# Transposes of norms and of A's outputs by the DMA engines, two residual buffers and an even split of Wo in a four-layer kernel

## The chip, the cores and the metric

The kernel runs on one core of one Trainium2 chip. The metric is the device time of one execution in microseconds; lower is better. Engines are named as in the profile: PE (TensorE matmul), PEld (its weight loads), DVE (VectorE), ACT (ScalarE), POOL (GpSimd), SP (SyncE, which only issues DMAs here). SPq and ACTq are the queues on which SP and ACT issue DMAs.

## The reference

A residual stream x of 2048 tokens and 640 channels passes through four layers, A, B, A, B, each after a layer norm without weights:

```python
x = A_x
x = x + _A_ref(_layernorm(x), A_wq, A_wk, A_wv, A_wo, A_beta)
x = x + _B_ref(_layernorm(x), B_mem0, B_Wq, B_Wk, B_Wv, B_Wo, B_seg_len)
x = x + _A_ref(_layernorm(x), A_wq, A_wk, A_wv, A_wo, A_beta)
x = x + _B_ref(_layernorm(x), B_mem0, B_Wq, B_Wk, B_Wv, B_Wo, B_seg_len)
```

Layer A has 32 heads of 20 channels and four segments of 512 tokens. In each segment every head does causal softmax attention inside the segment, and reads a memory M, z of the segments before through phi(q) M / (phi(q) z + 1e-6), with phi(t) = t + 1 for t > 0 and exp(t) else. A gate per head mixes the two; after that the segment's phi(k), v are added to the memory. The concatenated heads are multiplied by wo.

Layer B is recurrent: 64 steps of 32 tokens. A step puts 8 memory rows in front of its 32 tokens, projects all 40 rows to q, k, v of 32 heads of 128 channels, does masked softmax attention over the 40 rows, and multiplies by Wo (32 x 128 x 640). The first 8 output rows are the memory of the next step, the other 32 are the step's output. So step s + 1 cannot begin its memory part before step s has ended.

## The kernel before, in words

**Layer A** is cut into 32 units (4 segments n of 8 groups G of 4 heads), and each unit into six slots. In each slot PE computes a part of the scores (tile a_S), ACT takes exp into a_PT, POOL or DVE applies the causal mask to a_PT, and PE multiplies a_PT by the values (a_pv). Into the slots are woven the projections of the next unit (proj, tile a_PP, cast by DVE to a_qk), phi of q and k (phi_q, phi_k; k is turned by PE into a_KN), the memory update (memory), the normalisation of the unit before (norm, which writes 80 columns of the tile a_Onat, on DVE in the first segment and on POOL after it), and, in extras, work at fixed (G, slot) places. That work is: for the next segment, loading 128 rows of x (ln_load), their statistics (ln_stats), the norm (ln_apply, tile a_xn, one buffer), its transpose into a_xnT (ln_tr) and the value projection (vproj); for the segment before, the transpose of its outputs a_Onat into a_oT (chunk, five times) and the output projection (outp, eight times), which adds the residual and stores x in float32 and in bf16. One SBUF tile, a_wvo, holds wv and wo in turn. The PSUM pool pg of two buffers (tag "pg") serves proj, phi_k, memory, ln_tr, vproj, chunk and outp alike.

Both ln_tr and chunk transpose on PE: four or five 128x128 transposes into one PSUM tile, which ACT copies to SBUF.

**Layer B** works step by step. Its passes are Q and K of the memory columns (b_Qa, b_Ka, b_Qb, b_Kb), scores (b_SP), V (b_V), values (b_OTL) and the output pass OPass (b_OPS, 16 pairs of heads in HORDER: heads 0 to 15 first). The parts that do not depend on the memory are computed for four steps at once (TailUnit, tile b_tail; the deferred output pass b_OPSd) and are woven in as filling. The norm of the next 128 tokens is made once in four steps: ln_norm and ln_apply in a step with s % 4 == 2, ln_tr in the step after, again with five PE transposes (b_lntps) and an ACT copy into b_xnTg. The residual rows of a step are loaded into b_XO, one buffer, in the middle of the step; add_out adds the step's output to it on DVE, and store writes it out. For steps with s % 4 == 1 the store is made at the step's end, for the others in the middle of the next step.

Wo lies in two SBUF tiles: b_wo1 with the first NW1 = 11 heads, loaded at the beginning of layer B, and b_wo2 with the other 21, which takes space that layer A's output tiles (a_oT, a_wvo, a_xb and others) give free, and so is loaded after A's last output is stored. At the beginning of B the remaining output work of A (br.tail: the last chunk and eight outp) is woven between the first TailUnits and the first Q and K of step 0.

**Order.** PE, ACT, DVE and POOL execute in the order in which the program is written (the class _OrdNC chains each engine's instructions; its line 85 is therefore the source line of nearly all rows of the profile, and rows are told apart by tiles). DMAs issued through nc_raw.sync or nc.sync are not chained: their order on SP is the framework's scheduler's. The framework also inserts the waits for buffers and for memory that is used again.

## Time and profile before

| | us |
|---|---|
| median of 3 runs | 2297.86 |
| lowest and highest run | 2294.97, 2298.25 |
| profiled execution, its own time | 2302.5 |
| span of the profiled execution, first to last instruction | 2300.8 |
| first A, B, second A, second B (about) | 0 to 293, to 1140, to 1435, to 2301 |
| mean granted clock of TensorE | 0.981 |

A row of a group gives line, engine, operation, tile written <- tiles read (partitions x elements, type), count, then busy us, mean ns of one, and idle time of that engine just before, with what ended it. A row of the timeline gives start, length, engine and operation; in brackets stands the engine's idle time before it and what released it. A row of waits gives total us, number, longest. Matmuls overlap in PE's pipeline, so the duration of one is longer than the time that it costs; that time is read from the starts of two successors.

### The profile page before, as it was taken

The page shows a single profiled execution, that of the slowest core. Times are in us where ns is not written, and L with a number is a line of the kernel's source. Part 1 is how long each engine was busy: PE and PEld are TensorE (multiplying, and loading weights), DVE is VectorE, ACT ScalarE, POOL GpSimd, SP SyncE. Part 2 cuts the span into 40 slices and gives each one's busy share as a digit, 9 for nine tenths or more (in the row PEclk, how much of TensorE's full clock was granted, in tenths as well). Part 3 has the DMA queues.
Part 4 walks back from the last instruction along what each step waited for, and adds up shares of the span by engine and source line. Part 5 has one row for each costly group of instructions (what it writes and reads, how often), then busy time and mean ns, then how long its engine had stood idle before and what let it go on. Part 6 is the DMA issues. An engine that isn't in the chain of part 4 may idle for free.

```text
span 2300.8 us, 123029 instructions
## 1 busy us (share of the span) xinstructions
PE 2195.3 (95%) x54988; PEld 1234.9 (54%) x54988; DVE 1623.6 (71%) x3996; ACT 961.6 (42%) x2207; POOL 1028.5 (45%) x2475
## 2 busy tenths in 40 slices
PE   6998989999999999999889989899999999999997
PEld 3444545555555555555445445455555555555554
DVE  5777757777777777776667777577777777777775
ACT  5777823333333333333267667233323333333332
POOL 3344534444444444444323445344444444444442
PEclk9999989999999999999999999999999999999999
DMA  6455540000000000000123333400000000000000
GB/s 168 138 147 166 164 143 21 20 21 19 20 19 20 20 22 20 22 15 18 49 89 119 105 108 119 147 19 15 18 15 17 16 19 16 17 18 16 14 13 15
DMA packets 90652, 123.40 MB, mean 54 GB/s; under 512 B 16496, under 2 KB 80000, under 8 KB 88192
## 3 DMA queue, kind: packets, MB, share of 16 engines
q1 hardware_dynamic: 87648, 111.84, 16.9%
q8 instruction: 431, 7.06, 1.3%
q10 hardware_dynamic: 2464, 3.61, 0.6%
q14 instruction: 109, 0.89, 0.1%
HBM read 89.17 MB, written 26.21 MB: 50 GB/s over the span
## 4 chain that ended last, share of the span: by engine, by line
PE 81%; DVE 8%; ACT 5%; issue 3%; DMA 2%; SPq 1%; POOL 0%; DVEq 0%; ACTq 0%; POOLq 0%
PE b_V L85 13%; PE b_OPS L85 12%; PE b_tail L85 10%; PE b_Qa L85 6%; PE b_Kb L85 6%; PE b_Ka L85 6%; PE b_Qb L85 6%; PE b_SP L85 5%; PE a_PP L85 4%; ACT a_PT L85 4%; PE b_OTL L85 3%; PE b_OPSd L85 3%; PE a_S L85 2%; PE a_pv L85 2%; DVE a_qk L85 1%
## 5 line engine op out<-in xcount | busy, mean ns | idle before, releaser
L85 PEld LDWEIGHTS <-b_hT 128*32 128x32 bf16 x15120 | 372.3, 96 | 311.3 <-DVE b_hT L85 69.2
L85 ACT ACTIVATE b_PT<-b_SP 128x224 bf16<-128x224 f32 x256 | 92.3, 361 | 765.5 <-PE b_SP L85 744.7
L85 PE MATMUL b_V<-b_wv,b_hT 128*32 128x512 bf16 x5040 | 356.3, 381 | 0.0
L85 ACT ACTIVATE a_PT<-a_S 128x768 bf16<-128x768 f32 (+1 forms) x384 | 326.4, 893 | 62.8 <-PE a_S L85 56.1
L85 PE MATMUL b_OPS<-b_wo,b_OTsb 128*32 128x320 bf16 x8192 | 329.3, 302 | 6.5 <-DVE b_OTsb L85 5.1
L85 PEld LDWEIGHTS <-b_OTsb 128*32 128x32 bf16 x8192 | 200.4, 97 | 94.9 <-DVE b_OTsb L85 47.5
L85 POOL CAST b_QT<-b_TQ 128x384 bf16<-128x384 f32 x254 | 140.3, 552 | 231.5 <-DVE b_TQ L85 231.5
L85 ACT CAST b_OTsb<-b_OTL 128x320 bf16<-128x320 f32 x384 | 150.9, 427 | 198.9 <-PE b_OTL L85 183.1
L85 POOL TENSOR_TENSOR b_PT<-b_PT,b_R 128x64 bf16<-128x64 bf16 x256 | 107.3, 419 | 221.8 <-ACT b_R L85 197.4
L85 POOL CAST b_KT<-b_TQ 128x384 bf16<-128x384 f32 x254 | 142.6, 561 | 136.8 <-DVE b_TQ L85 132.1
L85 PE MATMUL b_Qa<-b_wq,b_hT 128*32 128x512 bf16 x2520 | 183.2, 384 | 5.0 <-DVE b_hT L85 5.0
L85 POOL TENSOR_SCALAR_AFFINE_SELECT a_PT<-a_PT 128x256 bf16<-128x256 bf16 x256 | 108.2, 424 | 174.2 <-ACT a_PT L85 162.1
L85 PE MATMUL b_Kb<-b_wk,b_hT 128*32 128x512 bf16 x2520 | 182.9, 380 | 0.1
L85 PE MATMUL b_Ka<-b_wk,b_hT 128*32 128x512 bf16 x2520 | 182.2, 382 | 0.0
L85 DVE STREAM_TRANSPOSE b_TM<-b_OPS 128x128 f32<-128x128 f32 x252 | 88.2, 350 | 123.6 <-PE b_OPS L85 119.7
L85 PE MATMUL b_Qb<-b_wq,b_hT 128*32 128x512 bf16 x2520 | 158.3, 379 | 0.0
L85 PE MATMUL a_PP<-a_xnT,a_wt 128*128 128x512 bf16 x560 | 146.5, 394 | 5.1 <-DVE a_um L85 1.3
L85 PE MATMUL a_S<-a_qk 32*128 32x512 bf16 (+3 forms) x1024 | 137.2, 308 | 8.1 <-ACT a_PT L85 6.9
L85 DVE CAST b_Vsb<-b_V 128x512 bf16<-128x512 f32 x128 | 88.6, 692 | 76.8 <-PE b_SP L85 48.0
L85 DVE CAST b_OTsb<-b_OTL 128x320 bf16<-128x320 f32 x128 | 62.9, 492 | 98.2 <-PE b_OTL L85 98.2
L85 DVE TENSOR_TENSOR b_PT<-b_PT,b_R 128x160 bf16<-128x160 bf16 x256 | 104.0, 406 | 37.7 <-PE b_V L85 18.6
L85 POOL TENSOR_TENSOR b_Rtot<-b_Rtot,b_R 128x160 bf16<-128x160 bf16 x256 | 126.6, 494 | 0.0
(165 smaller groups left out, 4276.0 us busy)
## 6 DMA issues: line engine op xcount, KB each, us to landing
a_wt<-a_wpad SPq DMA_DIRECT2D x112, 160.0 KB
b_XO<-xres SPq DMA_DIRECT2D x256, 30.0 KB
a_wvo<-in_A_wo_dram SPq DMA_DIRECT2D x8, 800.0 KB
b_wq<-in_B_Wq_dram SPq DMA_DIRECT2D x20, 256.0 KB
b_wk<-in_B_Wk_dram SPq DMA_DIRECT2D x20, 256.0 KB
xres<-a_xo SPq DMA_DIRECT2D x16, 320.0 KB
xres_bf<-a_xb SPq DMA_DIRECT2D x32, 160.0 KB
b_wv<-in_B_Wv_dram SPq DMA_DIRECT2D x20, 256.0 KB
```

Of the source, the lines that this page charges most:

```text
L85: r = f(*a, **k)
```

## The change

The norm's transposes of segments 1 to 3 of A, of the bridge between A and B, and of all of B, and the transposes of A's outputs become DMA transposes issued on SP; the first segment's norms and the transposes of k stay on PE. Loading, statistics, norm and transposes in A start one unit earlier (tt + 1 in place of tt + 2), the five calls of chunk become four of o_turn (one for each 128 tokens, at slots 3 and 4 of the segment's first unit), and outp is moved by about half a unit (from (1, 2) ... (3, 3) to (1, 3) ... (3, 5)). Several tiles go from one pool to another or from two buffers to one. exp of k is written into a_phik itself. B gets two b_XO buffers, loaded at the beginning of a step. NW1 goes from 11 to 16; the load of b_wo1 goes from SP, at B's beginning, to ACT's queue, after A's remaining output work. The first six TailUnits of B run without A's outputs between them, and two outp stand in front of each of the four first Q and K passes.

```diff
 S_TOK = 2048
-NW1 = 11
+NW1 = 16
...
         wk1 = ctx.enter_context(tc.tile_pool(name="a_wk1", bufs=1, reuse_waits="tile"))
+        nat = ctx.enter_context(tc.tile_pool(name="a_nat", bufs=1, reuse_waits="tile"))
...
         xnTs = [st.tile([128, NCH, 512], BF16, name=f"a_xnT{i}") for i in range(2)]
-        Onat = so.tile([128, 4, D], BF16, name="a_Onat")
+        Onat = nat.tile([128, 4, D], BF16, name="a_Onat")
...
 
-        def ln_tr(nc, xn, n, tt):
+        def ln_tr(nc, xn, n, tt, dma=True):
+            dst = xnTs[n % 2][:, :, 128 * tt:128 * tt + 128]
+            if dma:
+                nc_raw.sync.dma_start(dst, xn[:], transpose=True)
+                return
...
                 nc.tensor.transpose(tps[:, c, :], xn[:, 128 * c:128 * c + 128], C.identb[:])
-            nc.scalar.copy(xnTs[n % 2][:, :, 128 * tt:128 * tt + 128], tps[:])
+            nc.scalar.copy(dst, tps[:])
...
             nc.vector.memset(bd[32 * j:32 * j + 32, j, :], 1.0)
-        eps = so.tile([128, 2, 4, 4], F32, name="a_eps")
+        eps = st.tile([128, 2, 4, 4], F32, name="a_eps")
...
             if tt > 0:
-                ln_tr(nc, ln_apply(nc.vector, xts[tt - 1], *stats[tt - 1]), 0, tt - 1)
+                ln_tr(nc, ln_apply(nc.vector, xts[tt - 1], *stats[tt - 1]), 0, tt - 1, dma=False)
...
                 vproj(nc, 0, tt, half, ("dve", "act")[half])
-        gg = W.gates(nc, so)
+        gg = W.gates(nc, st)
...
             us, xin = {}, {}
-            wl = wk1 if general else wk
...
                 U = us[u]
-                t1 = wl.tile([128, 512], BF16, name="a_t1q", tag="t1")
+                t1 = wk1.tile([128, 512], BF16, name="a_t1q", tag="t1")
...
                 KNv = KN[:].rearrange("p t (j s) -> p t j s", s=32)[:, :, :, 0:20]
-                EK = wl.tile([128, 4, 4, 20], BF16, name="a_EK")
-                nc.scalar.activation(out=EK[:], in_=KNv, func=ACT.Exp)
-                t1 = wl.tile([128, 4, 4, 20], BF16, name="a_t1k", tag="t1")
+                pk = phik[u % 2][:, :, :, 0:20]
+                nc.scalar.activation(out=pk, in_=KNv, func=ACT.Exp)
+                t1 = wk1.tile([128, 4, 4, 20], BF16, name="a_t1k", tag="t1")
                 nc.vector.tensor_scalar(out=t1[:], in0=KNv, scalar1=1.0, scalar2=1.0, op0=ALU.add, op1=ALU.max)
-                nc.vector.tensor_tensor(out=phik[u % 2][:, :, :, 0:20], in0=EK[:], in1=t1[:], op=ALU.min)
+                nc.vector.tensor_tensor(out=pk, in0=pk, in1=t1[:], op=ALU.min)
...
                     nc.tensor.transpose(mt[:, qc, :], parts[:, qc].rearrange("p j i -> p (j i)"), C.identb[:])
-                ms = wl.tile([12, 512], BF16, name="a_ms", tag="t1")
+                ms = wk1.tile([12, 512], BF16, name="a_ms", tag="t1")
...
                 pv = us[u].pv
-                r = so2.tile([128, 2, 4, 4], F32, name="a_r")
+                r = wk.tile([128, 2, 4, 4], F32, name="a_r")
                 nc.vector.tensor_tensor(out=r[:, 0:K], in0=pv[:, 0:K, :, :, 20], in1=eps[:, 0:K], op=ALU.add)
-                i = so2.tile([128, 2, 4, 4], F32, name="a_i")
+                i = wk.tile([128, 2, 4, 4], F32, name="a_i")
...
                     watch(nc, C, r[:, 0].rearrange("p t j -> p (t j)"), i[:, 0].rearrange("p t j -> p (t j)"))
-                q = so2.tile([128, 2, 4, 4], F32, name="a_q")
+                q = wk.tile([128, 2, 4, 4], F32, name="a_q")
...
                 else:
-                    ts = so.tile([128, 2, 16, 20], F32, name="a_ts")
+                    ts = wk1.tile([128, 2, 16, 20], F32, name="a_ts")
...
                 else:
-                    um = wk1.tile([128, 4, 21], F32, name="a_um", tag="a_EK" if general else "a_um")
+                    um = wk1.tile([128, 4, 21], F32, name="a_um", tag="t1" if general else "a_um")
...
 
-            def chunk(c):
-                tps = pg.tile([128, 4, 128], BF16, name="a_otps", tag="pg")
-                for tt in range(4):
-                    nc.tensor.transpose(tps[:, tt, :], Onat[:, tt, 128 * c:128 * c + 128], C.identb[:])
-                nc.scalar.copy(oT[:, c, :], tps[:].rearrange("p t q -> p (t q)"))
+            def o_turn(tt):
+                nc_raw.sync.dma_start(oT[:, :, 128 * tt:128 * tt + 128], Onat[:, tt, :], transpose=True)
...
                     xn, m0 = ln["b"]
-                    tps = pg.tile([128, NCH, 128], BF16, name="a_btps", tag="pg")
-                    for c in range(NCH):
-                        nc.tensor.transpose(tps[:, c, :], xn[:, 128 * c:128 * c + 128], C.identb[:])
-                    nc.scalar.copy(br.xnT[:], tps[:])
+                    nc_raw.sync.dma_start(br.xnT[:], xn[:], transpose=True)
+                if (G, slot) == (6, 0):
+                    m0 = ln["b"][1]
+                    mp = wk1.tile([8, D], BF16, name="a_bm0p", tag="a_xn")
+                    nc.vector.tensor_copy(mp[:].rearrange("p (g jj d) -> p jj g d", jj=2, d=32),
+                                          m0[:].rearrange("p (jj g d) -> p jj g d", jj=2, d=32))
+                    ln["b"] = mp
+                if (G, slot) == (6, 3):
...
                     nc.gpsimd.tensor_copy(br.hT[:, :, 32:56], v[:, :, 1, 0:24])
-                    mp = wk1.tile([8, D], BF16, name="a_bm0p", tag="a_xn")
-                    nc.vector.tensor_copy(mp[:].rearrange("p (g jj d) -> p jj g d", jj=2, d=32),
-                                          m0[:].rearrange("p (jj g d) -> p jj g d", jj=2, d=32))
-                    ln["b"] = mp
...
                     if (G, slot) == (0, 0):
-                        chunk(3)
...
                             res_load(n - 1, 0); res_load(n - 1, 1)
-                    elif (G, slot) == (1, 0):
-                        chunk(4)
+                    elif (G, slot) in ((0, 3), (0, 4)):
+                        o_turn(2 * slot - 6); o_turn(2 * slot - 5)
                     else:
-                        seq = [(1, 2), (1, 3), (1, 5), (2, 0), (2, 3), (2, 5), (3, 0), (3, 3)]
+                        seq = [(1, 3), (1, 5), (2, 1), (2, 3), (2, 5), (3, 1), (3, 3), (3, 5)]
...
                     bridge_ops(G, slot)
-                seq = {(4, 0): 0, (5, 0): 1, (6, 0): 2}
-                if (G, slot) in seq:
-                    chunk(seq[G, slot])
...
                     for tt in range(4):
-                        if (G, slot) == (tt + 2, 0):
+                        if (G, slot) == (tt + 1, 0):
                             ln[tt] = ln_load(n + 1, tt)
-                        if (G, slot) == (tt + 2, 5):
+                        if (G, slot) == (tt + 1, 5):
                             ln[tt] = (ln[tt],) + ln_stats(nc, ln[tt])
-                        if (G, slot) == (tt + 3, 1):
+                        if (G, slot) == (tt + 2, 1):
                             ln[tt] = ln_apply(nc.vector, *ln[tt])
-                        if (G, slot) == (tt + 3, 4):
+                        if (G, slot) == (tt + 2, 4):
...
                     row_max(u + 1)
-            br.tail = [lambda: chunk(4)] + [lambda i=i: outp(NS - 1, i) for i in range(8)]
+            br.tail = [lambda i=i: outp(NS - 1, i) for i in range(8)]
...
             xn = ln_n.pop(g)
-            tps = pot.tile([128, NCH, 128], BF16, name="b_lntps", tag="ot")
-            for c in range(NCH):
-                nc.tensor.transpose(tps[:, c, :], xn[:, 128 * c:128 * c + 128], C.identb[:])
             xg = wk2.tile([128, NCH, 128], BF16, name="b_xnTg")
-            nc.scalar.copy(xg[:], tps[:])
+            nc.sync.dma_start(xg[:], xn[:], transpose=True)
...
         xnT_g[0], hT[0], hx[0] = br.xnT, br.hT, br.hx
-        for a, b in ((0, NW1 // 2), (NW1 // 2, NW1)):
-            nc_raw.sync.dma_start(wo[0][:, a:b, :], wo_src[:, a:b, :])
...
             nc.vector.memset(Rtot[:], 0.0)
-        XO = st.tile([64, 320], F32, name="b_XO")
-        nc.vector.memset(XO[:], 0.0)
+        XOs = [st.tile([64, 320], F32, name=f"b_XO{i}") for i in range(2)]
+        for t in XOs:
+            nc.vector.memset(t[:], 0.0)
...
                 flush()
-                if kind != "Q" or b:
-                    tail()
...
             for b in range(2):
+                tail(2)
...
                 place(("act", "pool")[b], turn(ps[:]), b, heads(dst[0]), 0, 24, 0)
-                tail()
         tail(100)
+        for a, b in ((0, NW1 // 2), (NW1 // 2, NW1)):
+            nc.scalar.dma_start(wo[0][:, a:b, :], wo_src[:, a:b, :])
...
         wo.append(wop2.tile([128, 32 - NW1, D], BF16, name="b_wo2"))
-        for a, b in ((NW1, 22), (22, 32)):
+        for a, b in ((NW1, 24), (24, 32)):
...
             T, i4 = divmod(s, 4)
+            XO = XOs[s % 2]
+            for jj2 in range(2):
+                nc.sync.dma_start(XO[32 * jj2:32 * jj2 + 24, :], x_src[32 * s:32 * s + 24, 320 * jj2:320 * jj2 + 320])
...
                 late.pop(0)()
-            for jj2 in range(2):
-                nc.sync.dma_start(XO[32 * jj2:32 * jj2 + 24, :], x_src[32 * s:32 * s + 24, 320 * jj2:320 * jj2 + 320])
...
                 ln_dma((s + 7) // 4)
-            def store(s=s, ops=ops):
+            def store(s=s, ops=ops, XO=XO):
```

## The prediction

> **What bounds the kernel now.** I read the page first, then busy time by stage, then the added and removed tiles one by one, then PE's waits, and last the chain of waits around the two places where a layer A hands over to a layer B. The page gives the span and the bound; the windows split it into layer A, B, A, B:
>
> ```profile
> span 2300.8 us, 123029 instructions
> PE 2195.3 (95%) x54988; PEld 1234.9 (54%) x54988; DVE 1623.6 (71%) x3996; ACT 961.6 (42%) x2207; POOL 1028.5 (45%) x2475
> ...
> 24.00:292.00 268.00, 244.83 (x2768) 130.18 (x2767) 196.36 (x502) 200.31 (x279) 120.94 (x309) 0.97 0.52 149
> 330.00:1138.00 808.00, 801.85 (x23918) 459.29 (x23922) 581.80 (x1418) 266.41 (x796) 374.78 (x897) 1.00 0.08 19
> 1166.00:1435.00 269.00, 245.47 (x2764) 130.23 (x2762) 196.62 (x487) 198.69 (x272) 116.73 (x281) 0.96 0.34 106
> 1476.00:2301.00 825.00, 806.56 (x24056) 465.52 (x24048) 585.30 (x1425) 268.21 (x800) 375.32 (x898) 0.99 0.07 16
> ```
>
> (Columns: stage, length, busy PE, PEld, DVE, ACT, POOL, clock, DMA share, GB/s.) In B, PE is busy 802 of 808 us: an operation taken off PE shortens B by its own length. In A, PE is busy 245 of 268; the other 23 us are short waits on DVE and ACT. So A is bound by PE first, and PE's waits second.
>
> What PE spends on the transposes that leave it, and what it waits in front of them:
>
> ```profile
> L85 PE MATMUL a_tps<-c_identb,a_xn x160: 216/219/315, 10.6 to 1369.4; 128*128 128x128 bf16 x160
> L85 PE MATMUL a_otps<-c_identb,a_Onat x160: 216/219/315, 58.2 to 1438.7; 128*128 128x128 bf16 x160
> L85 PE MATMUL b_lntps<-c_identb,b_xn x150: 218/219/231, 319.6 to 2177.4; 128*128 128x128 bf16 x150
> ...
> 2177.14 0.45 PE L85 MATMUL b_lntps<-c_identb,b_xn 128*128 128x128 bf16 x5
> 2177.53 0.40 PE L85 MATMUL b_V<-b_wv,b_hT 128*32 128x512 bf16 x4
> ...
> 268.29 0.39 PE L85 MATMUL a_otps<-c_identb,a_Onat 128*128 128x128 bf16 x4
> 268.61 0.33 PE L85 MATMUL a_S<-a_qk 32*128 32x384 bf16 x2
> ...
> PE a_otps L85 <- DVE a_vaug L85: 2.3, 6, 0.4
> PE a_tps L85 <- DVE a_vaug L85: 2.3, 4, 0.7
> ```
>
> The durations overlap; the start of the next instruction gives the price: five transposes hold PE for 2177.53 - 2177.14 = 0.39 us, four for 0.32.
>
> What the DMA engines do where the new transposes run:
>
> ```profile
> 1139.96 1.59 DMA b_XO<-xres
> ...
> 1456.17 2.51 DMA xres_bf<-a_xb
> 1459.29 12.72 DMA b_wo<-in_B_Wo_dram
> ...
> 1472.06 1.78 PE L85 MATMUL b_OPS<-b_wo,b_OTsb 128*32 128x320 bf16 x22 [1.28 <-DMA b_wo<-in_B_Wo_dram]
> ...
> 241.82 1.09 POOL L85 TENSOR_TENSOR a_Onat<-a_ts 128x320 bf16<-128x320 f32 x1
> ...
> 248.32 1.08 POOL L85 TENSOR_TENSOR a_Onat<-a_ts 128x320 bf16<-128x320 f32 x1
> ```
>
> A 160 KB transfer takes 2.51 us from issue to landing. The late part of Wo takes 12.7 us, and PE waits 1.28 us for it. Between the last write of a_Onat in one segment and the first of the next there are 248.32 - 242.91 = 5.4 us.
>
> **The change, part by part.**
>
> Transposes off PE. In A, three of four segments' norms go (12 groups of five per layer; the first segment's four stay on PE), so of 32 groups 24 go: 24 x 0.39 = 9.4 us. A's outputs: 160/4 = 40 groups x 0.32 = 12.8 us. The bridge's norm: 2 x 0.39 = 0.8. In B 30 groups x 0.39 = 11.7. Sum 34.7 us of PE, 23.0 in A and 11.7 in B. The Trainium skill (TensorE: Matmul & The Clock Gate, Part 4) puts a 128x128 transpose at 275 to 390 ns, which would make these 440 worth 121 us or more; here they follow each other at about 80 ns, and I take the trace's 34.7.
>
> ACT loses the copies behind them (0.58 us x 40, 0.69 x 54, about 60 us). ACT is not the bound, so they count nothing by themselves. But the transposes share two PSUM buffers (tag pg) with everything else in A, and PE stands in front of them: 2.3 + 2.3 + 1.3 us in the first A (also on a_xo), 3.4 + 1.5 + 1.3 in the second, 12.1 together. DVE is late for the next user of pg too, so I count half: 6 us; bounds 0 and 12.
>
> What is added: 24 + 32 + 2 + 30 = 88 DMA transposes of 128x640, all on SP's queue. No row shows one. From below, each is a plain 160 KB DMA: about 0.4 us of SP (a_wt's two issues take 0.8), landing after 2.5 us, and about 0.5 us behind a predecessor (160 KB at the 362 GB/s of the window 1461 to 1466, where Wo streams). From above, the Trainium skill (VectorE: DVE Perf Modes, The three transpose paths) gives 1309 ns for a 128x128 by DMA against 390 on TensorE, and this speaks against the change: five blocks make 6.5 us each (estimate). By the first, four transposes of A's outputs land after 2.5 + 3 x 0.5 = 4.0 us, inside the 5.4; by the second after 26 us, far outside. I take 1.2 us each behind a predecessor, nearer to the row, because a transfer spread over 16 engines should not serialise its blocks: 2.5 + 3 x 1.2 = 6.1 us.
>
> The waits that this adds. (a) The a_Onat tile has one buffer: the Onat addition of the next segment waits on POOL until all four transposes have read it. There are six such places, four of 5.4 to 5.9 us and two of 8.8 (after a first segment). Behind it on POOL stand the a_PT selects, for which the P*V matmuls wait. At 6.1 us POOL waits 0.5 us four times; its own 45% load hides this. (b) a_xn has one buffer: DVE's next norm waits for the transpose of the last. DVE writes a_xn at 195.14, 204.17 and 213.65, 9 us apart; the transpose may start within this time whenever SP is free, and SP's order has residual stores and loads in front of it. Mostly hidden; behind DVE stand the a_qk casts, and then PE. (c) The output projections start half a unit later, some 7 us after the transposes' issue: hidden. I put 3 us on (a) to (c) at PE. At 2.5 us instead of 1.2 it would be about 10 (the formula is under the first rival).
>
> In-place exp into phik, single t1 buffers, tiles moved between pools: written and read in the order of one engine or a unit apart; DVE and ACT orders hide them; nothing, at most 1 us. The bridge's POOL copies move from (5,4) to (6,3), still a unit before layer B: nothing.
>
> B's residual. With one b_XO buffer the load follows the last store; DVE waits 2.4 us for it in all (five times), and the chain of waits has its 1.59 us in front of the second A. Two buffers, loaded at the step's start, take both away: 3 us. SP's store-then-load wait stays, but hides.
>
> The hand-over. Before, 1,760 KB of Wo are issued at B's start and 3,360 KB after A's last outputs are stored. After, 2,560 KB go on ACT's queue behind A's last output projection and 2,560 on SP as before. So 5.2 MB are in flight at once; at 362 GB/s this is 14.5 us, beginning about a microsecond after the last projection: all of it lands about 16 us after, where it landed 15.6 to 17 us after before (1472 against 1454.7). The first half of the heads is whole in the first part, so the 1.28 us wait may go; but PE also stops 2.6 us for its own instructions in this load (1463.9 to 1466.5, "issue") and 3.4 us at 322, and two bulk queues may lengthen that. ACT's two issues (about 1 us) stand in front of the first b_PT exp, which comes 4 us later. POOL's copy to b_hx now waits for a transpose queued behind Wo on SP; POOL catches up while PE waits for Wo anyway. Net +1 us for both layers; bounds -3 and +10. A's last outputs are covered: four transposes land within some 9 us of the last Onat, and six tail units (3.97 + 4 x 1.19 us of PE) now run in front of the projections.
>
> Sum: 23.0 + 6 + 11.7 + 3 - 3 - 1 = 39.7 us saved. The profiled execution is 2302.5 us (span 2300.8), so 2262.8; it lies 4.6 above the median of the runs, 2297.86, so as a median 2258.
>
> **The rivals.**
>
> Slow transposes. If a DMA transpose takes t behind its predecessor, POOL is held 2.5 + 3t - 5.6 us at four places and 2.5 + 3t - 8.8 at two, less about 2 us of slack. The total is 18t - 37: with 6.5 us it is 80, plus some 15 for DVE's norms; against 43 us of gain the kernel takes about 2350. It turns slower from t = 4.4 us. For it: the skill's figure, the single a_Onat buffer. Against it: the rows of plain DMAs. A milder form, t near 3, costs 17 to 20 and gives 2275.
>
> A is not PE's. If DVE (196 of 268 us) and ACT set the unit's length, the 23 us on PE in A turn into waits on a_qk and a_PT, and only B's 11.7 + 3 and about 6 remain: 2277 too. For it: the rows of waits on DVE casts. Against it: PE's 91% in A.
>
> More than counted. All of the 12 us of waits vanish, and the half-clock stretches in A (clock 0.96 to 0.97) shrink: 34.7 + 12 + 4 + 10 = 61 us, 2237.
>
> **How the numbers follow.** Main case 0.58 (2246 to 2270), more 0.10, the two half gains 0.15, a gain eaten up to within 0.2% 0.05, slower 0.12. A measurement of this kernel tells about 0.2%, 4.6 us, from no change. The range 2234 to 2298 leaves out the slow case and the tail of the fast one. Faster by over 0.2%: 0.83.
>
> **What would show it.** Right: no a_otps and b_lntps rows, B's windows each about 6 us shorter with PE as busy, A's each 12 to 15 shorter, no wait on b_XO. Wrong: waits of POOL a_Onat or DVE a_xn on DMAs, PE b_OPS waiting on b_wo for more than 3 us, a longer PE "issue" at the hand-over, or SP issuing a transpose for over 2 us.

## The result, and the profile after

| | before | after |
|---|---|---|
| runs | 4 | 4 |
| median, us | 2296.49 | 2270.22 |
| lowest and highest, us | 2294.97 to 2298.25 | 2263.58 to 2272.96 |
| profiled execution: span (time), us | 2300.8 | 2271.2 (2272.96) |

The ratio of the medians is 0.9881 with an interval of 0.9856 to 0.9906: the changed kernel is faster by about 26 us. The page of its profile shows that TensorE has 440 matmuls fewer and is as full as it was, and that small packets have multiplied (before: 16496 under 512 B):

```profile
span 2271.2 us, 122201 instructions
PE 2150.9 (95%) x54548; PEld 1206.1 (53%) x54548; DVE 1632.1 (72%) x3998; ACT 907.9 (40%) x2111; POOL 1023.7 (45%) x2475
...
DMA packets 149785, 137.78 MB, mean 61 GB/s; under 512 B 75632, under 2 KB 139136, under 8 KB 147328
```

The stages say where the time came from. These are the windows with the same landmarks in both kernels: the two layers A, from the first matmul of a_PP to that of the last unit, and the two layers B, from the fourth step to the last. Columns: stage, length, busy PE, PEld, DVE, ACT, POOL, granted clock, DMA share, GB/s. First the kernel before:

```profile
24.57:280.42 255.85, 234.53 (x2627) 124.20 (x2625) 188.55 (x484) 189.63 (x265) 114.29 (x292) 0.97 0.54 153
1164.13:1422.34 258.21, 236.48 (x2626) 124.87 (x2625) 189.97 (x472) 187.38 (x259) 110.00 (x264) 0.97 0.35 110
360.90:1130.90 770.00, 764.88 (x22915) 439.47 (x22911) 557.09 (x1355) 255.41 (x762) 361.74 (x866) 1.00 0.08 20
1501.55:2274.94 773.39, 767.66 (x22915) 443.31 (x22911) 557.64 (x1355) 255.52 (x762) 361.70 (x866) 1.00 0.07 16
```

and the changed kernel:

```profile
25.32:269.79 244.47, 223.01 (x2494) 112.10 (x2492) 190.70 (x483) 173.80 (x235) 113.96 (x292) 0.98 0.69 174
1156.05:1388.10 232.05, 220.20 (x2494) 112.03 (x2492) 190.61 (x471) 171.50 (x229) 108.89 (x264) 1.00 0.52 140
356.38:1122.47 766.09, 760.26 (x22844) 439.16 (x22840) 560.20 (x1355) 247.07 (x748) 360.12 (x866) 1.00 0.10 23
1476.55:2242.48 765.93, 759.54 (x22845) 439.99 (x22841) 560.09 (x1355) 246.94 (x748) 360.02 (x866) 1.00 0.09 19
```

Four things are to be seen. The two B lose 3.9 and 7.5 us of length, and 12.7 us of busy PE together. The second A loses 26.2 us, of which PE's busy time gives 16.3 and its idle time 9.9 (258.21 - 236.48 = 21.7 before, 11.9 after), and its clock rises from 0.97 to 1.00. The first A loses only 11.4 us. These gains add up to 49.0 us, and the span fell by 29.6: so about 19 us were given back elsewhere. The place is the two hand-overs: from the last matmul of a_PP to the second step of B it takes 49.5 and 48.8 us before, 56.2 and 58.6 us after (+16.5). The other 3 us are at the end, the start and between the layers.

The new transposes themselves are as quick as the prediction assumed. The row of the tile a_oT (minimum, median, maximum of SP's issue in ns):

```profile
L493 SPq DMA_TRANSPOSE a_oT<-a_Onat x32: 1205/1276/2502, 90.9 to 1408.5; - x32
```

SP is held 1.28 us by each (median), where a plain load of the same size takes 0.43 us; four in a row go out 1.3 us apart, and the packets of the first at 285.40 end 1.9 us after its issue (packets of the trace, matched by time and size).

The waits that belong to the change (waiting engine and tile, what ended the wait, us in all, times, longest):

```profile
POOL a_xb L85 <- DMA xres_bf<-a_xb: 38.0, 9, 6.8
DVE a_st L85 <- DMA a_xt<-in_A_x_dram: 13.7, 6, 6.3
PE b_OPS L85 <- DMA b_wo<-in_B_Wo_dram: 9.7, 4, 4.2
PE b_Kb L85 <- DVE b_TQ L85: 9.5, 2, 6.3
POOL a_Onat L85 <- DMA a_oT<-a_Onat: 8.3, 4, 2.3
```

The wait of POOL on a_Onat is the one that the prediction named; PE waits only 0.6 us in all for POOL's a_PT, which stands behind it. No row of DVE's a_xn waiting for a DMA exists. The other four rows belong to what was given back; those of POOL and DVE count only where PE waits behind them. The chain of waits around the first hand-over tells their order (start, length, what):

```profile
303.63 6.38 DMA xres_bf<-a_xb
...
310.16 0.73 POOL a_xb L85
310.91 4.66 DMA xres_bf<-a_xb
...
316.22 10.60 DMA b_wo<-in_B_Wo_dram
...
326.86 1.28 PE b_OPS L85 x16
```

The third store of a_xb goes out at 303.63, just after ACT has issued 2.6 MB of Wo at 302.48. It lands late, POOL waits for the tile's one buffer, the last store comes later still, the second half of Wo may only start when that store has released the space (315.79), and PE stands in front of b_OPS until it is there. PE's other wait, 6.3 us for DVE's b_TQ, hangs on the same late store: on POOL the norm's b_ln_rstd stands behind a_xb, and DVE's b_xn, which waits for it, stands in front of b_TQ:

```profile
312.23 0.45 DVE L85 TENSOR_SCALAR b_xn<-b_xt,b_ln_mv,b_ln_rstd 128x640 bf16<-128x640 bf16 x1 [5.77 <-POOL b_ln_rstd L85]
```

In the first A there is one place more, here in the timeline:

```profile
157.47 6.28 SPq L493 DMA_TRANSPOSE a_oT<-a_Onat  x4
...
164.89 1.82 SPq L653 DMA_DIRECT2D b_wk<-in_B_Wk_dram  x4
166.76 0.42 SPq L248 DMA_DIRECT2D a_xt<-in_A_x_dram  x1
...
173.60 0.89 DVE L85 BATCH_NORM_STATS2 a_st<-a_xt 128x6 f32<-128x320 bf16 x2 [6.28 <-DMA a_xt<-in_A_x_dram]
...
175.55 0.60 ACT L85 ACTIVATE a_phiq<-a_PP 128x512 bf16<-128x512 f32 x1 [7.89 <-DVE a_qk L85]
```

Four transposes hold SP for 6.3 us, four loads of B's weights (256 KB each) follow, and only then the row block that the next norm needs. DVE waits 6.28 us for it, the cast of a_qk stands behind, and this unit takes 16.3 us where the same unit of the second A takes 9.3.

### The profile page after: what moved, and what is told of

It is laid out like the page before. It is cut to its first block, busy times and chain, and to the rows that moved or that the text cites. A ratio compares the mean times of both kernels' runs of the same rounds, so it can differ in the third digit from the quotient of the medians.

```text
span 2271.2 us, 122201 instructions
## 1 busy us (share of the span) xinstructions
PE 2150.9 (95%) x54548; PEld 1206.1 (53%) x54548; DVE 1632.1 (72%) x3998; ACT 907.9 (40%) x2111; POOL 1023.7 (45%) x2475
## 2 busy tenths in 40 slices
DMA packets 149785, 137.78 MB, mean 61 GB/s; under 512 B 75632, under 2 KB 139136, under 8 KB 147328
## 4 chain that ended last, share of the span: by engine, by line
PE 81%; DVE 7%; DMA 5%; ACT 3%; issue 2%; POOL 1%; SPq 1%; POOLq 0%; DVEq 0%; ACTq 0%
PE b_V L85 13%; PE b_OPS L85 13%; PE b_tail L85 10%; PE b_Kb L85 6%; PE b_Qa L85 6%; PE b_Ka L85 6%; PE b_Qb L85 6%; PE b_SP L85 5%; PE b_OTL L85 4%; PE a_PP L85 3%; PE b_OPSd L85 3%; ACT a_PT L85 2%; PE a_S L85 2%; PE a_pv L85 2%; DMA xres_bf<-a_xb 2%
## 5 line engine op out<-in xcount | busy, mean ns | idle before, releaser
L85 PE MATMUL a_PP<-a_xnT,a_wt 128*128 128x512 bf16 x560 | 141.8, 385 | 10.3 <-ACT a_phiq L85 6.2
L85 DVE STREAM_TRANSPOSE b_TQ<-b_Kb 128x512 f32<-128x512 f32 x128 | 91.7, 716 | 46.0 <-PE b_Kb L85 25.1
```

The source lines that it names most:

```text
L85: r = f(*a, **k)
```

## Experiments

The times of the whole kernel spread by 3 to 14 us within a set of runs, so most verdicts rest on stages of the profiled executions. How well those repeat can be seen from kernels in which a stage was not touched: the second A of the same code (first a_PP to last unit) took 232.0 to 235.4 us in ten executions, and the changed kernel's is the lowest of them; the two B (sum from fourth to last step) took 1531.7 to 1535.9, and the two hand-overs (sum from last a_PP to second step) 109.7 to 114.7 in the changed kernel and in E1, E3 and E4, which leave them alone; here the changed kernel's is the highest. A difference inside such a band proves nothing.

| run | ratio to before (interval) | first A | second A | hand-overs | B, sum |
|---|---|---|---|---|---|
| before | 1 | 259.4 | 261.7 | 98.3 | 1543.4 |
| changed | 0.9881 (0.9856 to 0.9906) | 247.7 | 235.2 | 114.7 | 1532.0 |
| e1_prefetch | 0.9879 (0.9847 to 0.9911) | 238.3 | 235.5 | 109.9 | 1531.7 |
| e6_order | 0.9905 (0.9870 to 0.9939) | 248.6 | 235.5 | 111.2 | 1532.6 |
| e7_wo_early | 0.9924 (0.9902 to 0.9946) | 249.1 | 238.1 | 118.4 | 1533.2 |
| e8_order_wo | 0.9920 (0.9888 to 0.9951) | 248.4 | 237.6 | 115.6 | 1533.2 |
| e10_wo_pieces | 0.9915 (0.9891 to 0.9939) | 250.1 | 237.9 | 115.9 | 1533.2 |
| e11_both | 0.9871 (0.9845 to 0.9896) | 246.4 | 238.1 | 112.8 | 1535.9 |
| e2_outputs_pe | 0.9944 (0.9923 to 0.9965) | 249.0 | 246.4 | 111.2 | 1535.1 |
| e3_norms_pe | 0.9983 (0.9972 to 0.9994) | 254.1 | 246.9 | 109.7 | 1534.2 |
| e4_b_norms_pe | 0.9924 (0.9896 to 0.9953) | 249.8 | 238.4 | 112.0 | 1543.4 |
| e5_one_xo | 0.9904 (0.9878 to 0.9931) | 249.2 | 237.5 | 109.2 | 1538.9 |
| e12_no_wo | 0.9804 (0.9777 to 0.9831) | 248.1 | 238.0 | 96.8 | 1534.2 |
| e13_old_handover | 0.9845 (0.9819 to 0.9872) | 243.3 | 237.2 | 115.0 | 1532.8 |

In this table A runs from the first to the last matmul of a_PP, which is 3.2 to 3.5 us more than to the start of the last unit, and the hand-overs begin there. (Landmarks of the expectations differ by that much; the numbers below say which is meant.)

**The parts, one at a time.** E2 and E3 put one of A's two kinds of transposes back on TensorE, E4 B's, E5 the single b_XO.

```
E2:  +def chunk(c): tps = pg.tile(...); 4 x nc.tensor.transpose(...); nc.scalar.copy(oT[:, c, :], ...)
     -    elif (G, slot) in ((0, 3), (0, 4)):  o_turn(2 * slot - 6); o_turn(2 * slot - 5)
     +    chunk(0), (1), (2) at (4, 0), (5, 0), (6, 0); chunk(3), (4) at (0, 0), (1, 0) of the next segment
E3:  -def ln_tr(nc, xn, n, tt, dma=True):
     +def ln_tr(nc, xn, n, tt, dma=False):
```

> The changed kernel, with the transposes of A's outputs back on TensorE in groups of four with their copies on ACT, as in the kernel before; norms stay with the DMA engines. In the second A (232.0 us changed, 258.2 before) some 17 groups return. Theory (their own time): 17 x 0.32 = 5.4 us of PE and 1 to 3 us of waits on the two pg buffers: the second A takes 238 to 241 us. Rival (clock and waits): the second A lost 26.2 us, of which transposes explain 10.5; PE's idle fell by 9.9 us and four stretches at half clock of 3.4 us each went. If outputs on PE bring these back, the second A takes 244 us or more and its clock falls from 1.00 to 0.98 or less. On the hand-overs: if the four transposes' 6.3 us on SP are what costs there, the stretches fall from 46.5/49.0 to 42 us or less; if Wo's block is, they stay at 44 or more.

> The changed kernel, with the transposes of A's norms for segments 1 to 3 back on TensorE in groups of five with their copies on ACT; outputs stay with the DMA engines. Theory (their own time): 12 x 0.39 = 4.7 us of PE and 3 to 5 us of waits (the kernel before waits 4.7 us in front of a_tps in the second A): it takes 239 to 242 us. Rival (clock and waits): 246 us or more, with half-clock stretches back. The two runs tell also whether the parts add up: with 26.2 us in all, two runs of 8 to 9 us each mean that 8 to 10 us come only when both are gone from the pg buffers. Hand-overs: no norms of A are turned there; the stretches stay at 45 to 50 us.

The second A, first a_PP to last unit, in E2 and in E3:

```profile
1155.05:1397.90 242.85, 228.53 (x2561) 118.63 (x2560) 190.72 (x471) 179.31 (x246) 109.51 (x264) 0.98 0.44 126
```

```profile
1159.96:1403.68 243.72, 227.26 (x2554) 116.36 (x2552) 190.24 (x471) 179.18 (x241) 109.80 (x264) 0.99 0.43 125
```

Against 232.05 these are 10.8 and 11.7 us more; against the slowest execution of the same code, 235.4, they are 7.4 and 8.3. The transposes' own time is 5.4 and 4.7 us, so each kind costs about one and a half to two and a half times that. Both lie between what the two theories expected. Part of the difference is waiting: PE is idle for 14.3 and 16.5 us, and for 11.9 in the changed kernel. In E3 PE waits 4.6 us in front of a_tps, as the kernel before did. The clock is less sure. The stage has 10.2 and 6.8 us at half clock, none in the changed kernel and 17.1 in five stretches before (not four, as the expectation says); but the other nine executions of the same code have 0 to 6.8, so what E3 shows may be chance. The two differences add up to 22.5 of the 26.2 us, or to 15.7 of 22.8 if 235.4 is taken for the changed kernel: 4 to 7 us come only when both are gone. In the first A, E2 is not longer than the changed kernel (249.0 and 247.7): without the transposes on SP it has no long unit, of which below, and against E1, which has none either, it is 10.7 us longer, as it is in the second (10.9). The hand-over sum of E2, 111.2, is inside the band; taking the transposes off SP there gave nothing that can be told.

```
E4:  -    nc.sync.dma_start(xg[:], xn[:], transpose=True)
     +    5 x nc.tensor.transpose(tps[:, c, :], ...); nc.scalar.copy(xg[:], tps[:])
E5:  -XOs = [... for i in range(2)]; the loads of XO at the start of a step
     +XOs = [... for i in range(1)]; the loads of XO behind the late stores, ahead of scores(1)
```

> The changed kernel, with layer B's norm transposes back on TensorE and their copies on ACT. In B, PE is busy 98% of the time, so the theory is that each returns its own 0.39 us: 30 x 0.39 = 11.7 us on the whole, 5.9 us in each B between its fourth and its last step (766.1 and 765.9 us in the changed kernel: 772). Rival: the DMA transposes cost PE something that the sum left out (the gain of 3.9 us measured in the first B is less than 5.9); then B grows by under 4 us in each layer.

> The changed kernel with one b_XO buffer and its loads late in the step, as in the kernel before. The prediction gave the second buffer 3 us on the whole. Theory: in B the addition of the output rows runs on DVE off PE's path; each B changes by less than 1 us and only the hand-overs differ, by 1 to 3 us less, since four loads leave SP's queue ahead of the first residual store. Rival: DVE's waits on b_XO (2.4 us in the kernel before) reach PE through b_TM; each B grows by 1.5 us or more.

E4's two B, fourth to last step:

```profile
357.94:1128.68 770.74, 764.50 (x22914) 437.64 (x22910) 557.37 (x1355) 255.26 (x762) 361.39 (x866) 1.00 0.08 19
1484.60:2257.28 772.68, 766.64 (x22914) 442.36 (x22910) 557.24 (x1355) 255.33 (x762) 361.41 (x866) 1.00 0.07 16
```

PE's busy time rises by 11.3 us (1519.8 to 1531.1), the length by 11.4, where the theory had 11.7. With B's own spread of 4 us the length tells 7.5 to 11.4; the agreement to 0.3 is closer than that allows, but the rival, under 4 us in each, fits only the lowest end of it. In E5 DVE waits for b_XO again (8.7 us in 6 places), and B is 6.8 us longer than in the changed kernel, 3 us longer than the longest untouched one (1535.9). That would be the rival's way rather than the theory's. But E4 and the kernel before differ in B by this buffer too, and take 1543.4 us both, so there it gave nothing. What the buffer is worth in B stays open, between 0 and 7 us; no row shows PE waiting for it.

**The long unit of the first A.** 

```
E1:  -                if pre and u % 2:
     +                if pre and u % NG >= 4:
```

> The changed kernel, with the loads of B's weights in the first layer A moved from every odd unit to the last four units of each segment (groups 4 to 7), where no output transposes are issued. In the changed kernel the first A is 12.4 us longer than the second (244.5 against 232.0, first a_PP to last unit), and one unit of it takes 16.3 us. Theory: the four 256 KB loads of b_wk stand between the four transposes and the load of a_xt on SP's queue, the load lands 6 us late, and DVE's statistics, its casts and then PE wait for it. Then the wait DVE a_st <- DMA a_xt (13.7 us in 6 places) falls under 3 us, the first A takes 234 to 238 us, and the whole is 7 to 10 us shorter than the changed kernel (about 2262 against 2270). Rival: what delays the load is the issue of the transposes themselves, 6.3 us of SP for four; the weights only stand by. Then the long unit keeps 13 us or more, the first A stays at 241 to 245 us, and the whole is within 3 us of the changed kernel.

First and second A, first a_PP to last unit:

```profile
24.48:259.59 235.11, 220.01 (x2493) 111.89 (x2492) 190.55 (x483) 173.70 (x235) 113.96 (x292) 1.00 0.70 176
1147.29:1379.58 232.29, 220.03 (x2493) 111.82 (x2492) 190.39 (x471) 171.60 (x229) 108.92 (x264) 1.00 0.52 140
```

The two A are now almost alike, the long unit takes 9.8 us, and DVE's longest wait for a row block falls from 6.3 to 2.1 us (7.7 in all, more than the 3 that was expected). So the loads of weights ahead of the row block were the cause of that unit. The clock goes with it: in the changed kernel and in eight others that have this unit, 6.8 us or more at half clock follow at 172 to 176 us; in E1, E11 and E13, which do not have it, there are none there. But the whole kernel did not become faster by an amount that can be told (0.9879), and in E11 and E13, which have the same edit, the first A took 8.1 and 5.0 us more than here. Half clock can account for that: E11 has 20.5 us of it there and E13 13.7, E1 none, and half of these times is 10 and 7 us. In the 7 us in front of E11's longest stretch, 10.2 us at 60.6, PE waits at most 0.4 us at a time; what sets such a stretch off stays open.

**The hand-overs.** E6, E7, E8 undo the order of the output projections, the place of the first part of Wo, and both; E10 cuts that part in four, and E11 adds E1's edit.

```
E6:  tail() behind each K and V tail unit and behind each first-step unit, in place of tail(2) ahead of each first-step unit
E7:  -    nc.scalar.dma_start(wo[0][:, a:b, :], ...)      behind tail(100)
     +    nc_raw.sync.dma_start(wo[0][:, a:b, :], ...)    ahead of ln_dma(1)
E8:  both
E10: -    two loads of 8 heads behind tail(100)
     +    nc.scalar.dma_start(wo[0][:, a:a + NW1 // 4, :], ...)    behind each tail(2)
E11: E10 and E1
```

> The changed kernel, with the output projections of A's last segment spread over the hand-over as in the kernel before: one after each of the four K and V tail units and one after each of the four first-step units, in place of two ahead of each first-step unit. Wo is loaded as in the changed kernel. From the first b_tail to the second step of B, the kernel before takes 39.8 and 39.2 us, the changed one 46.5 and 49.0 us: 16.5 us lost. Theory (order): pairs of projections back to back, with one a_xb buffer and residual rows that are loaded late, make POOL and PE wait. Then these stretches fall to 40 to 43 us and the whole is 9 to 14 us shorter than the changed kernel. Rival (Wo): what costs is that both halves of Wo are issued late and stand in front of the last stores, so that PE waits for b_wo 4 and 5 us at each hand-over. Then the stretches stay at 45 us or more, the waits on b_wo stay near 9 us in all, and the whole is within 4 us of the changed kernel. A second rival: the projections now come ahead of the transposes' landing and PE waits for a_oT instead, some 4 us at each hand-over, which leaves the stretches at 44 to 47 us.

> The changed kernel, with the first 16 heads of Wo issued on SP at the start of layer B, as the kernel before issues its first 11, in place of on ACT's queue behind the first-step units. The order of the projections stays that of the changed kernel. Theory (order): the pairs of projections cost the 16.5 us; then the stretches from first b_tail to second step stay at 45 to 49 us and the whole is within 4 us of the changed kernel, or longer, since 2.6 MB of Wo now stand in front of the first residual stores. Rival (Wo): the late Wo costs them; then the wait on b_wo is under 3 us in all, the stretches fall to 40 to 43 us and the whole is 8 to 14 us shorter than the changed kernel.

> The changed kernel with both: the projections spread as in the kernel before, and the first 16 heads of Wo issued on SP at the start of B. If order and Wo share the 16.5 us lost at the hand-overs, this gives back 12 to 16 us where each alone gives back about half: the stretches are 39 to 41 us, the whole 2254 to 2258. If order alone is the cause, it equals the run with the order alone within 3 us. If the loss is neither (the transposes' 6.3 us of issue on SP, or the loads of b_XO ahead of the first store), the stretches stay at 45 us or more in all three.

From first b_tail to second step E6 takes 45.5 and 46.5 us, E7 47.7 and 51.4, E8 46.6 and 49.9. Neither order nor place, nor both, gives the time back; E8's last case came true. Of the two causes that it names, E2 had none of the transposes on SP and stayed in the band, and E5, with two of the four b_XO loads out of the way, took 109.2, half a us under it. In E7 the wait has only moved. 2.6 MB of Wo now stand ahead of the first residual stores and of the residual rows that follow them, and PE waits in front of the projections:

```profile
PE a_YP L85 <- DVE a_xr L85: 9.9, 1, 9.9
PE a_YP L85 <- DVE a_xo L85: 8.6, 1, 8.6
```

> The changed kernel, with its first 16 heads of Wo issued on ACT's queue in four pieces of four heads, one with each first-step unit, in place of two pieces of eight behind them all. The three runs before left the stretch from first b_tail to second step at 45.5/46.5 us (order), 47.7/51.4 (early Wo) and 46.6/49.9 (both); the changed kernel has 46.5/49.0, the kernel before 39.8/39.2. Theory (collision): 2.6 MB of Wo in a block stand among the residual rows wherever they are issued; in the changed kernel the store of a_xb issued at 303.63 lands 5.5 us later in place of 1.9, POOL waits for it, DVE's b_TQ waits for POOL, and PE waits 6.3 and 3.2 us in front of b_Kb, then again for the second half of Wo. In pieces of 0.65 MB, the stores land within 3 us, the waits on b_TQ fall under 1 us, and the stretches are 40 to 43 us: 9 to 14 us less than the changed kernel's sum of 95.5. Rival (late start): SP is held 6.3 us by four transposes and then by ten small loads, so that all stores are late whatever Wo does, and a_xb has one buffer; then the waits on b_TQ stay above 3 us and the stretches at 44 us or more.

> The changed kernel with Wo in four pieces and with the loads of B's weights in groups 4 to 7 only: the two mends together. They touch different stages, so they should add up: the first A at 235 us (244.5 in the changed kernel), the two hand-over stretches at 81 to 86 us in all (95.5). Theory: 18 to 24 us shorter than the changed kernel, a ratio to the kernel before of 0.978 to 0.981. Rival: the pieces of Wo do nothing at the hand-overs; then only the first A is shorter, the ratio is 0.984 to 0.986.

In E10 the waits on b_TQ fall from 9.5 to 6.1 us and those on b_wo from 9.7 to 2.6, but PE waits up to 7.3 us in front of a_YP, where the changed kernel waits at most 4.2. The sum, 115.9, is that of the changed kernel, as E10's rival had it. Pieces do not help either, and E11's gain of 20 us over the changed kernel did not come (0.9871).

In five kernels the sum had stayed where it was. That pointed to the amount of traffic rather than to its order, and E12 took the amount away. It leaves out most of Wo: two heads of each half are loaded, and all heads are computed with these.

```
E12: -    return wo[0][:, h] if h < NW1 else wo[1][:, h - NW1]
     +    return wo[0][:, h % 2] if h < NW1 else wo[1][:, h % 2]
     and loads of one head each in place of eight
```

> The changed kernel, in which each half of Wo in layer B is loaded with two heads only, 0.33 MB each in place of 2.6 MB; all heads of a half are computed with these two, so this kernel leaves out most of Wo. Same instructions on every engine, same places of the loads. It measures what Wo's traffic costs at the hand-overs. From A's last unit to B's second step the kernel before takes 53.0 and 52.3 us, the changed one 59.3 and 61.8, the five attempts so far 56 to 64. Theory (traffic): without 4.6 MB of Wo the last residual stores land within 2.5 us of their issue, the waits of PE on b_TQ and b_wo go, and the stretches are 48 to 53 us, 16 us or more shorter in sum. Rival (late start and one a_xb): the four transposes and ten small loads hold SP for 10 us ahead of the first store, and each pair waits for the landing of the last a_xb store; then only the waits on b_wo (9.7 us) go, and the stretches are 54 to 57 us.

The hand-overs take 48.5 and 48.3 us from the last a_PP, 96.8 in sum: 17.9 less than in the changed kernel, 12.9 less than the shortest of the band, and 1.5 less than before. The sums over both, in the changed kernel, E12 and the kernel before:

```profile
sum 114.72, PE 81.41 PEld 41.38 DVE 49.59 ACT 28.26 POOL 41.79; mean PE 40.70 PEld 20.69 DVE 24.79 ACT 14.13 POOL 20.90
```

```profile
sum 96.83, PE 78.95 PEld 40.64 DVE 49.45 ACT 28.29 POOL 41.91; mean PE 39.47 PEld 20.32 DVE 24.72 ACT 14.14 POOL 20.96
```

```profile
sum 98.28, PE 83.51 PEld 40.51 DVE 49.21 ACT 31.81 POOL 40.62; mean PE 41.76 PEld 20.25 DVE 24.61 ACT 15.91 POOL 20.31
```

PE is idle for 33.3, 17.9 and 14.8 us: waiting makes 15.4 of the 17.9 us that E12 gains. The chain of its first hand-over has no wait on Wo and a third store of 3.4 us where the changed kernel had 6.4:

```profile
304.39 3.40 DMA xres_bf<-a_xb
...
311.13 1.04 PE b_Kb L85 x8
...
319.81 1.30 PE b_OPS L85 x32
```

The rival is not quite gone: PE still waits 5.5 us for b_TQ and 4.5 us in front of a_YP over the two hand-overs, in part from the late start and the one a_xb buffer. But the order, the 6.3 us of transposes on SP and the small loads are all still in E12, and with them alone the hand-overs are as short as before, though that kernel had all of Wo to load. E12 takes away two things at once, PE's own waits on b_wo (9.7 us) and what the traffic does to stores and residual rows; it does not tell what a smaller cut would give. How full the DMA engines are (second number from the end) in 42 us of the first hand-over, changed kernel and E12:

```profile
285.00:327.00 42.00, 28.15 (x544) 14.51 (x540) 16.41 (x34) 6.04 (x16) 12.01 (x23) 0.91 0.74 208
```

```profile
285.00:327.00 42.00, 34.62 (x692) 17.66 (x688) 21.03 (x48) 6.49 (x18) 15.73 (x32) 0.94 0.40 100
```

In the kernel before the share is 0.58 in the like stretch (293 to 335 us), with 1.8 MB of Wo issued and mostly loaded in the 9 us between the first b_tail (293.6) and the first residual store (302.5). The last question was whether that place is still free.

```
E13: E1 and E6, and
     NW1 = 11; the early part of Wo with nc.scalar.dma_start ahead of the tail units
     Onat = so.tile(...) in place of nat.tile(...)
```

> The changed kernel with the kernel before's hand-over, but for the transposes: projections one after each unit, a_Onat kept with the other output tiles so that the first part of Wo no longer takes its space, 11 heads of Wo early and 21 late, the early part on ACT's queue ahead of the tail units; also B's weights loaded in groups 4 to 7 only. All transposes of the change by the DMA engines and the two b_XO buffers stay. Theory (place of Wo): 1.8 MB of Wo start at A's last P*V, beside the transposes, and have landed before the first residual store, as they had in the kernel before; stretches from A's last unit to B's second step of 53 to 56 us (59.3 and 61.8 changed), the first A at 235 to 243 us, the whole 2250 to 2256 us where the kernel before takes 2297: a ratio of 0.980 to 0.982. Rival (transposes on the way): the oT transposes now share the DMA engines with Wo and land 5 us later, and the spread projections wait for them; stretches stay at 58 us or more, ratio 0.985 to 0.988.

```profile
279.21 6.95 SPq L492 DMA_TRANSPOSE a_oT<-a_Onat  x4
279.22 0.96 ACTq L85 DMA_DIRECT2D b_wo<-in_B_Wo_dram  x2
...
285.37 1.52 PE L85 MATMUL a_YP<-a_wvo,a_oT 128*128 128x320 bf16 x5 [3.10 <-DMA a_oT<-a_Onat]
```

and in its chain of waits

```profile
279.21 6.11 DMA a_oT<-a_Onat
```

It is not free: transposes and Wo now start together, what PE needs of a_oT lands 6.1 us after the first issue (9.3 at the second hand-over), and PE waits 3.1 us at the first hand-over and 6.4 at the second. The late part of Wo then costs 5.6 us in front of b_OPS at the first and 5.3 at the second. The hand-overs' sum is 115.0: the rival. The ratio, 0.9845, is the lowest of the complete kernels, but its interval overlaps the changed kernel's, the two were not run side by side, and its profile gives the credit to the first A. It is not shown to be faster. The kernel that would settle the place was not run: Wo early as here, with A's outputs transposed on TensorE and the rest of the change.

## Why the prediction was right, and where it was wrong

The forecast was faster, 2258 us, with a range of 2234 to 2298; the median is 2270, and the saving on the profiled execution is 29.6 us where the sum had 39.7. The terms behind it were further off than the total.

- **B's transposes, 11.7 us: right.** E4 gives back 7.5 to 11.4. The price from the starts of neighbouring rows (0.39 us for five) holds because PE is busy over 99% of these steps. So the trace's 80 ns for each transpose stands against the 275 to 390 ns of the Trainium skill (TensorE: Matmul & The Clock Gate, Part 4), as the prediction chose.
- **The speed of the DMA transposes, 1.2 us behind a predecessor: right in size, in part by luck.** They go 1.3 us apart. But the 1.2 was put between 0.5 and 6.5 as a time of the DMA engines, and what spaces them is SP's own time: the prediction's lower end had 0.4 us for it, the row has 1.28, while the packets of one pass in 0.7 us (286.58 to 287.32 for the first at 285.40). The estimate of 6.5 us from the Trainium skill (VectorE: DVE Perf Modes, The three transpose paths) would have put this change on the slow side, and no row here shows such a spacing: four of them hold SP for 6.3 us in all.
- **A's transposes and waits, 23 + 6 - 3 = 26 us: too small.** The two A gave 11.4 + 26.2 = 37.6. The term for waits in front of transposes was halved on the thought that DVE is late for the next user; PE's idle time in the second A fell by 9.9 us, not by 3. The granted clock stood in the third rival (10 us) and not in the sum: the second A of the kernel before has five stretches of 3.4 us at half clock, which are worth up to 8.5 us of PE, and the changed one has none. As other executions of the same code have up to 6.8 us of them, how much of this the change brings is open. E2 and E3 bring the waits back in part.
- **Waits (a) to (c), 3 us:** (a) is 2.1 us in each of four places and not 0.5, hidden as argued; (b) does not exist. What was not seen is the row block behind four transposes and four weight loads on SP, 6.5 us in one unit (E1). The prediction named residual stores and loads in front of the transposes; the wait that came is behind them.
- **b_XO, 3 us: open.** E5 speaks for 3 to 7 us in B, E4 against the kernel before for nothing. The two terms of B came to 14.7 us, and B became 11.4 shorter, which B's spread of 4 us allows.
- **The hand-over, a cost of 1 us with bounds of -3 to +10: the step that failed.** It cost 16.5 us, and 11 to 14 in E1, E3, E4 and E5. The prediction had both parts of Wo in flight at once and all of it landed about 16 us after the last projection. They came one behind the other. The last projection (changed kernel, first hand-over) starts its last matmul at 302.3:

```profile
L85 PE MATMUL a_YP<-a_wvo,a_oT x40: 296/299/311, 290.6 to 302.3; 128*128 128x320 bf16 x40
```

The first part is issued at 302.48, and the second could only be issued at 315.79, when the last store had landed, and lands at 326.82: 24.5 us after the projection. In the kernel before, SP issues its late part 3.8 us after the last matmul of a_YP, at 313.5:

```profile
317.28 1.42 SPq L915 DMA_DIRECT2D b_wo<-in_B_Wo_dram  x2
```

And the sum priced Wo's loads only by PE's waits on b_wo (9.7 us), not by the stores and residual rows that come late beside them, for which PE waits 9.5 us at b_TQ and 6.7 at a_YP. E12 shows that all of the loss goes when most of Wo goes. Why there is no good place left for Wo is argued, not shown: the kernel before loaded the first part in 9 us ahead of the residual stores, and there the transposes run now; E13 shows the waits that come when both do. PE waiting over 3 us for b_wo stood among the signs that would prove the forecast wrong, but was not sized; of the others, SP issuing a transpose for over 2 us came too (up to 3.1), a longer "issue" of PE did not.

A's terms were too small by 11.6 us, the hand-over's too favourable by 15.5 and B's by 3.3, and 3 us went at the ends. That the total came within 12 us of the forecast is in part luck: errors of opposite sign cancelled. The rival of slow transposes did not happen; the total lies near the one in which A gives little (2277), for a different reason.

## What to carry to other kernels

Taking transposes off a full TensorE paid about their spacing in the trace, and in the stage where TensorE also waits, one and a half to two and a half times that. Before a queue gets new transfers, look at the stretch where it is fullest and list every transfer that the program already needs there: here the sum no longer fitted, and reordering and cutting only moved the wait. And count the issuing engine's own time: whatever stands behind the new instructions in its order is late by that much.

## What the runs showed that was not expected

- A DMA transpose of 128x640 bf16 (160 KB) holds SP for 1.2 to 1.3 us, three times a plain load (0.43), and up to 3.1 us behind 2.6 MB of Wo. Alone it lands 1.9 us after its issue; of four beside a 1.8 MB load, what PE needs lands 6.1 and 9.3 us after the first issue (E13).
- The changed kernel moves 59,000 more packets under 512 B (75,632 against 16,496; E4 has 55,473), but B's length shows no cost of them: E4 without its 30 transposes is longer by what PE does for them.
- The granted clock halves for 3.4 us or multiples of it, in different places in kernels with the same code: the second A of like code had 0 to 6.8 us of such stretches, the first 0 to 20. One follows the long unit's wait of PE (6.2 us, then 6.8 us at half clock from 172.9); but in front of none of the five in the second A of the kernel before is PE idle for more than 0.9 us at a time, in the 7 us that precede it. The clock goes with a part of the spread between runs of one kernel: in E3's 20 runs the mean granted clock goes from 0.981 to 0.971 and the time from 2285.2 to 2299.1 us, with a correlation of -0.82.
